# Top-k attention with a gated feed-forward: four units transposed by TensorE instead of by DMA

## The chip, the cores and the metric

One Trainium2 chip, one core. The metric is device time in microseconds (us), the median of three runs. The profile is one further execution, taken by the hardware profiler; its times are counted from the start of its span.

## The reference, cut to what matters

```python
# q, k, v: (8, 8, 576, 64);  w_in: (512, 2048);  w_out: (2048, 512)
scores = scale * q @ k.T
kth = np.partition(scores, -32, axis=-1)[..., -32:-31]   # 32nd largest of 576
scores = np.where(scores >= kth, scores, -1e9)
attn = exp(scores - max) ; attn = attn / (attn.sum + 1e-9)
x = (attn @ v).transpose(0, 2, 1, 3).reshape(4608, 512)
h = x @ w_in
out = (h * cos(h)) @ w_out
```

The two weight matrices arrive as 64-bit floats. The kernel reads them as pairs of 32-bit integers and decodes them itself.

## The kernel before, in words

**Units and slots.** The 4608 tokens are cut into 36 blocks of 128. For each block there are four *units*, one per pair of heads (NP is 4): 144 units. The main loop runs one *slot* per unit. In slot `i` three units are at work: `u` (unit i) is searched for its top 32 values, `w` (unit i-1) is masked and exponentiated, and `x` (unit i-2) is transposed. Every second slot, two older units `z` are multiplied with V.

**What each engine does in a slot.** VectorE folds the 576 scores to two halves (`fold_high`, L260) and runs eight rounds of MAX8 and MATCH_REPLACE8 (L352, L357); this is its main work. GpSimd makes the other half of the fold (L276, L285). For unit numbers in `BUSY` it does not: there VectorE makes it with one more instruction (`fold_now`, L268). Late in the slot VectorE takes the sum (L397) and the reciprocal (L402) of unit w's exponentials, which ScalarE made (mask L381, exponentials L389). ScalarE also copies the next unit's scores from PSUM (L248, and L252 for the last 128 columns, which lie in a tile called `rim`).

**Transposing a unit.** P@V needs the probabilities with the keys on the partitions. `send` does that by way of DRAM: `split` lets GpSimd rewrite the unit as 16-bit halves (L412) together with the reciprocals spread over 128 columns (L414), `write_halves` writes 640 KB to DRAM on SyncE's queue (L422), and `transposes` reads it back with a DMA transpose (L428) into `pT`. There is one `halves` buffer. `values` then makes P@V on TensorE (L447) into columns 256 to 383 of `rim`, and `take_values` multiplies it by the transposed reciprocals on VectorE (L455) into `xT`.

**Feed-forward.** When the four units of a block have their `xT`, the block's feed-forward may start: 8 pieces of the first product (`ff1`, L504) and 8 of the second (`ff2`, L579), 576 pieces in all. Between them stand two ScalarE reads of each bank (L518, L520), a range reduction on GpSimd (L540, L549), a sine on ScalarE (L559) and a gate on GpSimd (L566). `feed` hands pieces to TensorE between the attention products, about four a slot, limited by a credit. After the last slot only feed-forward work of the last blocks is left.

**Weights.** The 32 weight chunks of 512 KB are loaded during the first slots into staging buffers (seven of tag `g`, shared with the feed-forward, and three of tag `x`). Each is decoded in three steps: two ScalarE instructions at the end of a slot (L133, L136), one on VectorE in the next slot (L144), one on GpSimd behind it (L154), which frees the staging buffer. A piece may be issued only if the chunks that it needs were decoded in an earlier slot.

**Order.** Nothing is rescheduled: each engine's instructions stand in the order in which the program issues them, and each engine and each DMA queue works through its own in order. Slot 0 starts with L260 at 7.40 us; the start of a slot below is always the start of its L260.

Of the kernel before, what the change touches and what calls it, by code (L numbers as in the profile page):

```python
# [10 lines left out]
F32 = mybir.dt.float32  # L11
# [6 lines left out]
P = 128  # L18
# [12 lines left out]
def kernel(  # L31
# [9 lines left out]
    nc = tc.nc  # L41
    ctx.enter_context(tc.manual_schedule())
    B, H, D, S = qT.shape
    DM, DF = moe_w_in.shape
    NT = S // P
    TAIL = S - NT * P
    MAIN = NT * P
    NP = H // 2
# [8 lines left out]
    work = ctx.enter_context(tc.tile_pool(name="work", bufs=2))  # L57
    small = ctx.enter_context(tc.tile_pool(name="small", bufs=4))
    ps = ctx.enter_context(tc.tile_pool(name="ps", bufs=2, space=bass.MemoryType.PSUM))
# [3 lines left out]
    ident = consts.tile([P, P], F32, tag="ident")  # L63
# [15 lines left out]
    NC = DM // P  # L79
# [12 lines left out]
        w_out.append(w)  # L92
        chunks.append((moe_w_out[f * P : (f + 1) * P, :], w))
    CHUNKS, XB = 7, 3
    BUSY = range(7, 12)
    ff = {"live": 0, "tick": 0, "now": 0, "credit": 0.0, "end": False, "kind": 0, "half": 0, "open": 0, "late": False}

    wq = {"next": 0, "loaded": deque(), "second": deque(), "third": deque(), "done": 0, "ready": 0}
# [1 line left out]
    def staged(spare=0):  # L100
        return sum(c[2] == spare for k in ("loaded", "second", "third") for c in wq[k])

    def load_weights(n, queue):
        for _ in range(n):
            i = wq["next"]
            if i >= len(chunks):
                return
            src, dst = chunks[i]
            if not DECODE:
                queue.dma_start(out=dst, in_=src)  # L110
                wq["next"] = wq["done"] = i + 1
                continue
            spare = i < 3 * XB and i % 2 == 1 and staged(1) < XB
            if spare:
                st = ffw.tile([P, CW, 2], I32, tag="x", name="st", bufs=XB)
            elif staged() + ff["live"] >= CHUNKS:
                return
            else:
                st = ffw.tile([P, CW, 2], I32, tag="g", name="st", bufs=CHUNKS)
            queue.dma_start(out=st.rearrange("p w i -> p (w i)"), in_=src)  # L120
            wq["loaded"].append((st, dst, int(spare)))
            wq["next"] = i + 1
# [38 lines left out]
    units = []  # L161
# [61 lines left out]
    rim = ps.tile([P, 2, 512], F32, tag="rim", name="rim", bufs=1)  # L223
    sc_ends = [rim[:, :, i * (S - SB) : (i + 1) * (S - SB)] for i in range(2)]
    room = [rim[:, j, 2 * (S - SB) :] for j in range(2)]
# [28 lines left out]
    def fold_high(u):  # L254

        s, sc = u["s"], u["sc"]
        if u["n"] not in BUSY:
            del u["sc"]
# [5 lines left out]
    def fold_now(u):  # L264

        s, sc = u["s"], u.pop("sc")
        u["low"] = work.tile([P, 2, HS], F32, tag="low", name="low", bufs=1)
        nc.vector.tensor_tensor(  # L268
            out=u["low"], in0=sc[:, :, 0:HS], in1=s[:, :, HS:S], op=ALU.min
        )  # L270

    def fold_sum(u):

        s = u["s"].bitcast(I32)
        u["low"] = work.tile([P, 2, HS], F32, tag="low", name="low", bufs=1)
        nc.gpsimd.tensor_tensor(  # L276
            out=u["low"].bitcast(I32), in0=s[:, :, 0:HS], in1=s[:, :, HS:S], op=ALU.add
        )

    def fold_low(u):  # L280

        if u["n"] in BUSY:
            return
        low = u["low"].bitcast(I32)
        nc.gpsimd.tensor_tensor(  # L285
            out=low, in0=low, in1=u["rest"][:, :, HS:S].bitcast(I32), op=ALU.subtract
        )
# [15 lines left out]
    def topk_first(u, w):  # L303

        u["top"] = tops[u["n"] % len(tops)]
        if w:
            merge_first(w)
        if u["n"] not in BUSY:
            fold_sum(u)
        fold_high(u)  # L310
        if w:
            merge_second(w)
        if u["n"] in BUSY:
            fold_now(u)
        topk_round(u, 0, [lambda: bounds(w), lambda: distances(w)] if w else ())
# [21 lines left out]
    def merge_first(u):  # L337
        n = TOPK // 2 + 1
        u["lesser"] = u["top"].rearrange("p j r i -> p j (r i)")[:, :, 2 * n : 3 * n]
        nc.vector.tensor_reduce(  # L340
            out=u["lesser"], in_=u["top"][:, :, 0:n], axis=mybir.AxisListType.X, op=ALU.min
        )

    def merge_second(u):
        nc.vector.tensor_reduce(
            out=u["top"][:, :, TOPK - 1, 1], in_=u.pop("lesser"), axis=mybir.AxisListType.X,
            op=ALU.max,
        )
# [58 lines left out]
    def split(u):  # L407


        s = u.pop("s").rearrange("p j k -> p (j k)").bitcast(U16)  # L410
        halves = work.tile([P, 2, 2 * S + P], U16, tag="halves", name="halves", bufs=1)
        nc.gpsimd.tensor_copy(out=halves[:, :, 0 : 2 * S], in_=s.rearrange("p (k h) -> p h k", h=2))  # L412
        rden = u.pop("rden").bitcast(U16).rearrange("p (j h) -> p h j", h=2)
        nc.gpsimd.tensor_copy(  # L414
            out=halves[:, :, 2 * S :].rearrange("p h (j d) -> p h j d", j=2),
            in_=rden.unsqueeze(3).to_broadcast([P, 2, 2, D]),
        )
        u["halves"] = halves

    def write_halves(u):  # L420
        rows = u["rows"] = dram.tile([P, 2, 2 * S + P], U16, tag="rows", name="rows")
        nc.sync.dma_start(out=rows, in_=u.pop("halves"))  # L422

    def transposes(u):
        rows = u.pop("rows").rearrange("q h k -> (q h) k")
        pT = u["pT"] = work.tile([P, 2 * NT + 2, P], F32, tag="pT", name="pT", bufs=3)
        words = pT.rearrange("p c q -> p (c q)").bitcast(U16)
        nc.sync.dma_start_transpose(  # L428
            out=words.rearrange("p (c q) -> p c q", c=2 * NT + 2), in_=rows
        )  # L430
# [95 lines left out]
    def take_banks():  # L526
        while full:
            take, *what = full.popleft()
            take(*what)
# [22 lines left out]
    def sines(least):  # L552

        n = sum(c[3] < ff["now"] for c in waiting)
        if n == 0 or (n < least and waiting[0][3] + 2 > ff["now"]):
            return
        for _ in range(n):
            blk, g, x, _ = waiting.popleft()
            nc.scalar.activation(out=x, in_=x, func=AF.Sin, bias=halfpi, scale=TWO_PI_BELOW)  # L559
            sined.append((blk, g, x))  # L560
# [88 lines left out]
    at_slot, at_once = {}, {}  # L649
# [7 lines left out]
    for n in range(NP, len(order)):  # L657
        i = last[order[n - 6]] if n >= 6 else 0
        load_at(max(i, 2 * NP + 2), load_qk, *order[n])
        i = last_values[order[n - 6]] if n >= 6 else 0  # L660
        load_at(max(i + 4 - i % 2, 2 * NP + 2), load_v, *order[n])

    for hp in range(NP):
        at_once[hp] = [(load_v, 0, hp)]
    for hp in range(2, NP):
        at_once[hp - 2].append((load_qk, 0, hp))


    for i, u in enumerate(units):
# [2 lines left out]
    def send(x):  # L672

        split(x)
        write_halves(x)
        transposes(x)

    def slot(i, u, w, x, z):
        n = (3, 4, 3, 2)[i] if i < NP else 2 if i < 2 * NP else 3
        if i < NP:  # L680
            for load, b, hp in at_once[i]:
                load(b, hp)
        load_weights(n, nc.sync if i < 2 else nc.scalar)
        if x:
            send(x)
        decoding = i < 3 * NP
        ff["late"] = False
        topk_first(u, w)
        fold_low(u)
        topk_round(u, 1)  # L690
        topk_round(u, 2)
        if decoding:
            sines(1)
            gate(1)
        decode_second(NP)
        decode_third()
        reduce_first()
        reduce_second()
        made = scored.get(i, [])
        if z:  # L700
            take_banks()
        feed(1)

        for m in made:
            scores(m)
        if z:
            values(z)


        late = len(made) > 0  # L710

        if i % 2 and not decoding:
            sines(1)
        if w:
            mask(w)
        take_banks()
        if w and late:
            exponentials(w)
        if i + 1 < NU:
            take_scores(units[i + 1])  # L720
        if w and not late:
            exponentials(w)
        topk_round(u, 3, both(w), z)
        ff["late"] = not decoding
        if i in at_slot:
            load, b, hp = at_slot[i]
            load(b, hp)
        gate(1)
        feed(1 if len(made) == 2 else 2)
        take_banks()  # L730
        decode_first(NP)
        reduce_first()
        reduce_second()
        feed(1 if len(made) == 2 else 3)
# [31 lines left out]
    tt = ps.tile([P, 512], F32, tag="mm", name="warm", bufs=2)  # L766
# [8 lines left out]
    for i in range(NU):  # L775
        ff["credit"] = min(ff["credit"] + 5.0 - 0.9 * len(scored.get(i, [])), 5.3)
        ff["now"] += 1
        wq["ready"] = wq["done"]
        u, w, x = (units[i - n] if n <= i else None for n in range(3))
        z = units[i - 4 : i - 2] if i % 2 == 0 and i >= 4 else None  # L780
        slot(i, u, w, x, z)
    ff["end"], ff["late"] = True, False
    drain(units[NU - 1], units[NU - 2], units[NU - 4 : NU - 2])
# [42 lines left out]
```

## Time and profile before

| | |
|---|---|
| median of 3 runs | 1442.53 us (1441.97 to 1443.62) |
| the profiled execution's own time | 1443.18 us |
| its span, first to last instruction | 1441.4 us |
| mean granted TensorE clock | 0.993 |
| TensorE busy | 1371.2 us (95%) |
| VectorE busy | 1359.3 us (94%) |
| GpSimd busy | 1166.3 us (81%) |
| ScalarE busy | 1089.5 us (76%) |

Busy shares of the whole span mix three stages: a start of some 170 us in which weights are loaded and decoded and little feed-forward work is there, a long even stretch, and a last stretch of some 60 us with feed-forward work alone. Each has to be read by itself. The starts of the first slots in this execution, read from VectorE's timeline:

| slot | 0 | 1 | 2 | 3 | 4 | 5 | 6 | 7 |
|---|---|---|---|---|---|---|---|---|
| start, us | 7.40 | 17.22 | 27.21 | 37.66 | 48.34 | 63.01 | 72.67 | 82.73 |

| slot | 8 | 9 | 10 | 11 | 12 | 13 | 14 | 15 |
|---|---|---|---|---|---|---|---|---|
| start, us | 93.03 | 105.14 | 115.77 | 128.69 | 139.32 | 149.18 | 159.96 | 169.35 |

### The profile page before, as it was taken

The numbers are of one execution on the slowest core, as the hardware profiler recorded it, in microseconds if no ns is written. First come the engines' busy times: TensorE is split into PE (matmuls) and PEld (weight loads), VectorE is DVE, ScalarE is ACT, GpSimd is POOL, SyncE is SP. The second block draws the span as 40 slices with busy tenths as digits, with TensorE's granted clock in tenths as the row PEclk, the third lists the DMA queues.
The fourth block names the chain that finished last, engine by engine and source line by source line (L and its number), as shares of the span: only waits on it lengthen the run. The fifth ranks groups of instructions, "written<-read, shape, count | busy, mean of one in ns | idle before, by whom it ended". The sixth has DMA issues, their size and how long they took to land.

```text
span 1441.4 us, 30146 instructions
## 1 busy us (share of the span) xinstructions
PE 1371.2 (95%) x10252; PEld 978.4 (68%) x10252; DVE 1359.3 (94%) x5237; ACT 1089.5 (76%) x1910; POOL 1166.3 (81%) x816
## 2 busy tenths in 40 slices
PE   4387899999999999999999999999999999999998
PEld 3164677777777777777777777777777777777765
DVE  7899999999999999999999999999999999999931
ACT  7577787777777788777877777777877778777742
POOL 6876888888888888888888888888888888888820
PEclk9989999999999999999999999999999999999999
DMA  8877676666666566657665566756665656655530
GB/s 288 254 216 208 184 199 175 156 167 184 187 154 151 152 191 187 163 143 189 185 168 153 148 187 177 179 154 161 196 186 152 140 169 170 167 143 151 154 99 15
DMA packets 438379, 245.25 MB, mean 170 GB/s; under 512 B 386384, under 2 KB 403024, under 8 KB 438224
## 3 DMA queue, kind: packets, MB, share of 16 engines
q1 hardware_dynamic: 429648, 222.13, 57.6%
q10 hardware_dynamic: 8576, 21.19, 4.2%
q8 instruction: 81, 1.33, 0.4%
q14 instruction: 74, 0.61, 0.1%
HBM read 45.09 MB, written 103.81 MB: 103 GB/s over the span
## 4 chain that ended last, share of the span: by engine, by line
PE 88%; DVE 7%; ACT 3%; DMA 1%; SPq 0%; POOL 0%; issue 0%; ACTq 0%; POOLq 0%
PE mm L504 34%; PE o L579 33%; PE rim L447 11%; PE sc L238 8%; DVE top L352 3%; PE rim L238 2%; DVE rest L357 2%; DMA rows<-halves 1%; DVE rest L260 1%; ACT s L381 0%; DVE low L357 0%; ACT s L389 0%; SPq L428 0%; DVE w_out L144 0%; DMA pT<-rows 0%
## 5 line engine op out<-in xcount | busy, mean ns | idle before, releaser
L504 PEld LDWEIGHTS mm<-xT,w_in 128*128 128x128 f32 x4608 | 536.9, 192 | 76.4 <-issue 64.7
L504 PE MATMUL mm<-xT,w_in 128*128 128x128 f32 x4608 | 539.2, 275 | 8.0 <-ACT x L520 4.8
L579 PE MATMUL o<-w_out,g 128*128 128x512 f32 x1152 | 537.4, 600 | 9.4 <-POOL w_out L154 5.3
L352 DVE MAX8 top<-rest 128x8 f32<-128x288 f32 x1152 | 478.9, 451 | 0.0
L412 POOL COPY halves<-s 128x2304 uint16<-128x2304 uint16 x144 | 303.1, 2105 | 159.2 <-ACT s L389 153.4
L357 DVE MATCH_REPLACE8 rest<-top,rest 128x288 f32<-128x288 f32 x864 | 376.6, 443 | 0.0
L579 PEld LDWEIGHTS o<-w_out,g 128*128 128x128 f32 x1152 | 202.7, 190 | 197.3 <-issue 186.5
L352 DVE MAX8 top<-low 128x8 f32<-128x288 f32 x576 | 243.9, 449 | 2.7 <-POOL low L285 2.6
L389 ACT ACTIVATE s<-s,nd 128x576 f32<-128x576 f32 x288 | 220.2, 767 | 0.8
L285 POOL TENSOR_TENSOR low<-low,rest 128x576 int32<-128x576 int32 x139 | 197.2, 1418 | 10.9
L381 ACT ACTIVATE s<-s,top 128x576 f32<-128x576 f32 x288 | 206.0, 765 | 0.0
L276 POOL TENSOR_TENSOR low<-s 128x576 int32<-128x576 int32 x139 | 196.6, 1414 | 5.0 <-ACT s L252 5.0
L238 PE MATMUL sc<-k,q 64*128 64x448 f32 (+1 forms) x640 | 150.1, 588 | 35.4 <-DVE rest L260 16.3
L518 ACT ACTIVATE g<-mm 128x512 f32<-128x512 f32 x144 | 85.9, 596 | 118.0 <-PE mm L504 115.8
L549 POOL TENSOR_TENSOR x<-g,x 128x1024 f32<-128x1024 f32 x68 | 160.9, 2365 | 5.7
L566 POOL TENSOR_TENSOR g<-g,x 128x1024 f32<-128x1024 f32 x68 | 161.0, 2368 | 0.0
L447 PE MATMUL rim<-pT,v 128*64 128x128 f32 (+1 forms) x2560 | 148.6, 270 | 0.0
L447 PEld LDWEIGHTS rim<-pT,v 128*64 128x64 f32 x2560 | 130.8, 140 | 12.5 <-issue 11.3
L248 ACT COPY s<-sc 128x896 f32<-128x896 f32 x144 | 129.2, 898 | 3.6 <-PE sc L238 3.2
L252 ACT COPY s<-rim 128x256 f32<-128x256 f32 (+1 forms) x160 | 60.8, 380 | 90.2 <-PE rim L447 90.0
L357 DVE MATCH_REPLACE8 low<-top,low 128x288 f32<-128x288 f32 x288 | 125.5, 444 | 0.0
L260 DVE TENSOR_TENSOR rest<-sc,s 128x576 f32<-128x576 f32 x144 | 107.7, 748 | 6.3 <-ACT s L252 6.3
(47 smaller groups left out, 1196.9 us busy)
## 6 DMA issues: line engine op xcount, KB each, us to landing
rows<-halves SPq DMA_DIRECT2D x144, 640.0 KB, 3.0
out_dram<-ob ACTq DMA_DIRECT2D x36, 256.0 KB, 2.2
q<-in_q_dram SPq DMA_DIRECT2D x31, 288.0 KB, 3.4
v<-in_v_dram SPq DMA_DIRECT2D x32, 256.0 KB, 3.3
st<-in_moe_w_out_dram ACTq DMA_DIRECT2D x16, 512.0 KB, 4.6
st<-in_moe_w_in_dram SPq DMA_DIRECT2D x10, 512.0 KB, 5.4
k<-in_k_dram SPq DMA_DIRECT2D x31, 144.0 KB, 3.3
k<-in_k_dram SPq DMA_DIRECT2D x32, 128.0 KB, 3.4
```

The costliest lines, as they stand in the source:

```text
L238: nc.tensor.matmul(to[r0 : r0 + rows, rim_bank(r0, j) if k0 else place(u["hp"], j), 0 : k1 - k0], st["q"][d, q0 : q0 + rows], st["k"][d, k ...
L276: nc.gpsimd.tensor_tensor(out=u["low"].bitcast(I32), in0=s[:, :, 0:HS], in1=s[:, :, HS:S], op=ALU.add)
L285: nc.gpsimd.tensor_tensor(out=low, in0=low, in1=u["rest"][:, :, HS:S].bitcast(I32), op=ALU.subtract)
L352: nc.vector.max(to[:, j], src[:, j])
L357: nc.vector.match_replace(rest[:, j], to[:, j], src[:, j], NEG)
L381: nc.scalar.activation(out=s[:, j], in_=s[:, j], func=AF.Prelu, bias=less[:, j, 1:2], scale=1.0, alpha=FAR)
L389: nc.scalar.activation(out=s[:, j], in_=s[:, j], func=AF.Exp, bias=nd[:, j : j + 1], scale=SCALE, accum_out=den[:, j, 0:1],)
L412: nc.gpsimd.tensor_copy(out=halves[:, :, 0 : 2 * S], in_=s.rearrange("p (k h) -> p h k", h=2))
L447: nc.tensor.matmul(room[i][d, r], lhsT, rhs, start=c == NT, stop=c == NT - 1)
L504: nc.tensor.matmul(mm[:, at : at + w], w_in[f // FC][:, c, (f % FC) * P : (f % FC + 1) * P], blk["xT"][:, c], start=c == 0, stop=c == NC - 1,)
L566: eng.tensor_tensor(out=g, in0=g, in1=x, op=ALU.mult)
L579: nc.tensor.matmul(o, g[:, at : at + P], w_out[f], start=f == 0, stop=f == NF - 1)
```

## The change

Units 0 to 3 are no longer sent through DRAM. A new function `turn` lets TensorE transpose them into PSUM (nine 128x128 transposes) and makes the spread, transposed reciprocals as two products with the identity; ScalarE copies the results to `pT` in three instructions. `turn` runs in slots 2 to 5, in `send`'s place; `send` starts with unit 4 in slot 6. P@V of units 2 and 3 is made in slot 5 instead of slot 6. The weights go on SyncE's queue up to slot 5 (before: slot 1), and the numbers of chunks a slot are raised: with three ahead of the loop, the chunks whose VectorE step falls in slots 0 to 12 are 3, 3, 4, 3, 2, 2, 2, 2, 2, 3, 2, 3, 1 before and 3, 3, 4, 4, 3, 4, 3, 2, 2, 2, 2, 0, 0 after. The loads of V for the first four head pairs move from slots 0 to 3 to slots 2 and 3. Unit 11 leaves `BUSY`.

```diff
-    BUSY = range(7, 12)
+    BUSY = range(7, 11)
...
-            spare = i < 3 * XB and i % 2 == 1 and staged(1) < XB
+            spare = i < 2 * NC + 10 and i % 2 == 1 and staged(1) < XB
...
+    def turn(u):
+
+        s = u.pop("s").rearrange("p j k -> p (j k)")
+        pT = u["pT"] = work.tile([P, 2 * NT + 2, P], F32, tag="pT", name="pT", bufs=3)
+        for half in range(2):
+            tt = ps.tile([P, 512], F32, tag="mm", name="tt", bufs=2)
+            for c in range(NT):
+                at = (half * NT + c) * P
+                nc.tensor.transpose(tt[:, c * P : (c + 1) * P], s[:, at : at + P], ident)
+            nc.scalar.copy(out=pT[:, half * NT : (half + 1) * NT], in_=tt.rearrange("p (c q) -> p c q", c=NT))
+        at = 2 * NT * P
+        nc.tensor.transpose(room[0][:, P : 2 * P], s[:, at : at + P], ident)
+        rden = u.pop("rden")
+        for j in range(2):
+            lhsT = rden[:, j : j + 1].to_broadcast([P, D])
+            nc.tensor.matmul(room[1][j * D : (j + 1) * D, P : 2 * P], lhsT, ident, start=True, stop=True)
+        nc.scalar.copy(out=pT[:, 2 * NT :], in_=rim[:, :, 3 * P :])
...
-        at_once[hp] = [(load_v, 0, hp)]
+        at_once.setdefault(hp // 2 + 2, []).append((load_v, 0, hp))
     for hp in range(2, NP):
-        at_once[hp - 2].append((load_qk, 0, hp))
+        at_once[hp - 2] = [(load_qk, 0, hp)]
...
-        n = (3, 4, 3, 2)[i] if i < NP else 2 if i < 2 * NP else 3
+        n = (3, 4, 4, 3, 4, 3)[i] if i < NP + 2 else 2
...
-        load_weights(n, nc.sync if i < 2 else nc.scalar)
+        load_weights(n, nc.sync if i < NP + 2 else nc.scalar)
         if x:
-            send(x)
+            (turn if i < NP + 2 else send)(x)
...
         z = units[i - 4 : i - 2] if i % 2 == 0 and i >= 4 else None
+        if NP < i < NP + 3:
+            z = units[2:4] if i == NP + 1 else None
```

## The prediction

> **What bounds the kernel now.** I read the page's busy shares, then the chain that ended last, then a table by stretches cut at slot starts, then VectorE's waits and each engine's timeline in the first 170 us.
>
> ```profile
> PE 88%; DVE 7%; ACT 3%; DMA 1%; SPq 0%; POOL 0%; issue 0%; ACTq 0%; POOLq 0%
> ...
> 48.30:63.00 14.70, 7.21 (x48) 5.07 (x48) 10.48 (x40) 5.69 (x12) 11.23 (x9) 1.00 0.86 233
> 63.00:72.70 9.70, 1.82 (x8) 0.84 (x8) 9.70 (x39) 7.11 (x15) 6.29 (x6) 0.61 1.00 336
> 169.30:1370.00 1200.70, 1199.94 (x9163) 858.83 (x9163) 1187.62 (x4626) 945.43 (x1652) 1035.09 (x709) 1.00 0.62 168
> ```
>
> The columns of the last three are stretch, length, then busy time of TensorE, its weight loads, VectorE, ScalarE, GpSimd, then clock, DMA share and GB/s. From 169.3 to 1370 us TensorE is busy 1199.94 of 1200.70 us: it is the bound, and VectorE has 13 us to spare. Before 169 us TensorE has long gaps, and VectorE runs through: slot 5 is 9.70 of 9.70. Only slot 4 breaks that, 10.48 of 14.70. So two rules: a saving on TensorE before slot 14 is worth nothing by itself, and a VectorE stall there moves the moment from which TensorE never rests again. Comparing the two programs' orders on TensorE, 25 feed-forward pieces stand ahead of slot 14's P@V in both, and the order is the same from there to the end. The last stretch therefore holds the same work; what the change gives is how much earlier slot 14 starts (159.96 us now).
>
> The stalls on VectorE from slot 0 to 13:
>
> ```profile
> 43.40 2.27 POOL L285 TENSOR_TENSOR low<-low,rest 128x576 int32<-128x576 int32 x1
> ...
> 52.02 2.10 POOL L412 COPY halves<-s 128x2304 uint16<-128x2304 uint16 x1 [2.63 <-DMA rows<-halves]
> ...
> 57.69 0.82 DVE L352 MAX8 top<-low 128x8 f32<-128x288 f32 x2 [2.03 <-POOL low L285]
> ...
> 61.56 0.49 DVE L455 TENSOR_TENSOR xT<-rim,pT 128x128 f32<-128x128 f32 x2 [2.19 <-ACT s L252]
> ...
> 61.15 0.37 ACT L252 COPY s<-rim 128x256 f32<-128x256 f32 x1 [7.22 <-PE rim L447]
> ...
> 56.80 0.69 PE L447 MATMUL rim<-pT,v_tail 64*64 64x128 f32 x4 [4.75 <-DMA pT<-rows]
> 57.42 3.68 PE L447 MATMUL rim<-pT,v 128*64 128x128 f32 x32
> ...
> 89.01 0.75 DVE L144 TENSOR_SCALAR w_out<-w_out 128x512 int32<-128x512 int32 x2
> ...
> 122.04 2.99 DVE L144 TENSOR_SCALAR w_out<-w_out 128x512 int32<-128x512 int32 x2
> ...
> 122.22 2.53 POOL L566 TENSOR_TENSOR g<-g,x 128x1024 f32<-128x1024 f32 x1
> ```
>
> Slot 4 is the DRAM trip: the write of `halves` was late behind loads, so GpSimd waited 2.63 for the one buffer, its fold was late, and VectorE waited 2.03; then the DMA transpose held TensorE 4.75, P@V was late, L252 stands behind it, and VectorE waited 2.19. The last three lines are a hidden stall: two L144 take 0.75, but 2.99 while GpSimd's gate runs. Adding up: slot 3 0.57 (L285), slot 4 4.22, slot 8 1.33 (1.17 hidden in L144), slot 10 2.24, slot 12 0.13, slot 13 1.52 (L397 behind ScalarE): 10.0 us.
>
> **The change part by part.**
>
> *VectorE's own work.* The same 32 chunks and ten `xT` products up to slot 13; unit 11 leaves `BUSY`, one L268 less, 0.66 by the step between its neighbours. So gain = 0.66 + 10.0 - S, with S the stalls of the new order. Bare slots: 9.0 (slot 14: 9.39 with 0.40 for `xT`), plus 0.33 a chunk, 0.40 with `xT`, 0.66 in `BUSY`.
>
> *Removed.* Four L412/L414 pairs on GpSimd (2.5 us each), four 640 KB writes and transposes, so SyncE no longer stands 7 us on a write in slots 2 and 3. The stalls of slots 3 and 4 lose their causes.
>
> *Added: turn.* Neither the transposes of `s` nor the products with the identity are in the trace. Nearest rows: the 12 warm-up transposes, 2.82 us, 0.235 each; P@V cold, 3.68/32, two records a product, 0.23; ScalarE's L518 (512 columns from PSUM, 0.48 step) and L252 (256 columns, 0.27). Nine and two make 2.6 us on TensorE, three copies 1.25 on ScalarE. Lower bound: nothing exposed (a gain is excluded, it is extra work); upper: all 3.9 in each of four slots, 15 us. I step it. The products wait for L402, the end of the slot before; the last copy is then done some 1.2 us into the slot, and the mask behind it waits for VectorE's L372, 1.7 us into it. ScalarE's slot is 4.0 (mask 1.43, exponentials 1.53, copies 1.06) plus 1.12 a chunk plus 1.25: 9.7 with four chunks, under VectorE's 10.3. Cover: VectorE; without it, 1.25 a slot.
>
> *A rule against it.* The trace has P@V at 1.97 us when TensorE had been busy and 3.68 when not, though the granted clock is printed as 1.00 in both. The Trainium skill, "TensorE: Matmul & The Clock Gate", Part 4: PE-mode transpose, says that transposes do not count as busy for the clock gate. By that rule P@V behind `turn` stays cold, 4.3 with its tails; if transposes warmed the array, 2.3. The sums differ by S in slot 5: 0.7 against none. No row here decides; I take cold.
>
> *Loads.* Up to slot 5 some 16 MB on SyncE's queue. The kernel moves 321 to 357 GB/s in slots 0 and 1. The V loads stand behind weights and Q/K and land by 40 us, wanted at 52. Chunk 17 waits for a staging buffer freed by L154 of slot 3 (about 48.7); four chunks at 260 GB/s land by about 58, and ScalarE wants them from 57.5 to 61. Cost nothing, cover 2 to 3 us. Later chunks on ScalarE's queue wait for buffers freed earlier.
>
> *Stepped by hand from slot 4.* Start 48.1 = 7.40 + 9.82 + 9.99 + 10.45 + 10.11 + 0.33. Slot 5 at 58.5 (three chunks, `xT`).
> Slot 4: TensorE cold: products 0.5, scores 5.0, P@V 4.3 from 48.0, say 57.5 to 57.8; L252, four chunks (4.5), copies: 63.5. Slot 5: P@V until 67.8 (VectorE wants it at 68.1), L252 and exponentials 69.6, L397 wants them at 68.9: 0.7. Slot 6 at 69.9.
> Slot 6: GpSimd makes four L154 until 70.5, L412/L414 until 73.0, folds until 75.9; L144 comes at 75.5 and waits 0.4. Two bank reads stand ahead of the exponentials, so L252 ends at 80.6: 0.4 more. Slot 7 at 80.7.
> Slot 7: three L154 until 80.8, L540 and L549 until 84.2, L412/L414 until 86.6, the first gate until 89.0. L144 comes at 87.0: 2.0. Slot 8 at 93.0.
> Slot 8: the second product waits for that gate; five pieces of 1.8 (the chain has 32 records of L504, two pieces, in 3.57) from 89.0 to 98.0 (99.5 if cold), scores and P@V to 102.9 or 104.4, wanted at 102.3: 0.6 to 2.1, I take 1.3.
> Slot 9: gate about 108.4 to 110.8, L144 at 111: 0.3. Slots 10 to 13: no gate beside L144, the sine of slot 13 not late: none.
> S = 0.7 + 0.8 + 2.0 + 1.3 + 0.3 = 5.1. Gain 5.6; slot 14 at 154.4.
>
> *The second rule.* L144 at 2.99 beside L566, and L285 stretched from 1.41 to 2.27 beside L144. The skill's "SBUF — State Buffer", SBUF: two separate sides, says that GpSimd and a two-port VectorE instruction hold a port pair exclusively for a whole instruction, whoever starts first. By the rule each L144 that starts inside any GpSimd instruction waits for its end: 0.4 + 2.0 + 0.3. Were only the gate's collisions real, 2.3. The rows bear the rule out; since arrivals are known to about 1 us, slots 6 to 9 together could be 0 to 6.
>
> *The sum.* 1443.18 - 5.6 = 1437.6 for the profiled execution, whose median lies 0.65 lower: 1437.0.
>
> **The rivals.**
> *Collisions and waits eat the gain.* The first gate comes a slot earlier, and chunks are packed three and four a slot, so GpSimd is behind in slots 6 and 7 (12.5 us of work in slot 6). If slots 6 to 10 meet a GpSimd instruction at full length and slot 13 keeps its 1.5, S is 8 to 13 and the time 1440 to 1445. For it: two of five L144 groups beside feed-forward work were hit before. Against: that takes nearly every one.
> *Cleaner than stepped.* L144 falls between GpSimd's instructions and the array is warm: S about 2, 1433.8. Against: the gate follows `split` directly, 4.9 us of GpSimd without a hole.
> *Slower: weights late in front of turn.* In slots 4 and 5 ScalarE's order is chunks, copies, mask, L252 behind P@V, exponentials, and VectorE's L397 waits for the last. Every us that chunk 20 lands after 61 is a us of stall. It is slower by 0.2% (2.9 us) only from S above 10.7 + 2.9, some 13.5, 8.4 more than stepped: chunk 20 would have to land after about 69.5, 2.1 MB in 21 us or 100 GB/s. For it: all loads in one queue, each waiting for a staging buffer. Against: 336 GB/s in slot 5 before.
> *The change doesn't do what it says:* the orders show that it does.
>
> **How the numbers follow.** As stepped, S 3 to 7.8: 0.66. Cleaner, S below 3: 0.14. Eaten, S 7.8 to 13.5: 0.13. Slower: 0.07. About 2.9 us (0.2%) is what a measurement of this kernel can tell from no change. The likeliest time is 1437.0. The range, 1433.5 to 1441.0, is S from 1.6 to 9.1. Faster 0.80, same 0.13, slower 0.07.
>
> **What would show it.** Right: slot 5 starts near 58.5 and slot 14 near 154.4; no wait for L285 in slots 3 and 4; L144 long in slot 7. Wrong: L397 or `xT` waiting several us in slots 5 to 8; ScalarE waiting for staging loads after 50 us; TensorE idle after slot 15, which would show that the shift is not kept to the end.

## The result and the profile after

| | before | after |
|---|---|---|
| median of 7 runs each, same chip | 1442.83 us (1441.97 to 1449.78) | 1438.23 us (1436.85 to 1439.10) |
| ratio, after to before | | 0.9960, 95% interval 0.9943 to 0.9976 |
| profiled execution, its own time | 1443.18 us | 1438.41 us |
| its span | 1441.4 us | 1436.6 us |
| start of slot 5 | 63.01 us | 58.41 us |
| start of slot 14 | 159.96 us | 154.32 us |

The change makes the kernel faster by 0.3 to 0.4%: the quotient of the two medians is 0.9968, and the ratio in the table, 0.9960, is that of the means, into which one run of 1449.78 us before enters. In the experiments, too, the ratio can differ from the quotient of the medians, by up to 0.0005. The forecast, 1437.0 within 1433.5 to 1441.0 and faster with 0.80, holds.

The new kernel is 18 lines longer behind `turn`: P@V is now L465 (before: L447), `xT` L473 (L455), the first product L522 (L504), the gate L584 (L566), the second product L597 (L579), the write to DRAM L440 and the DMA transpose L446.

The same views as before. The chain that ended last, in shares by engine:

```profile
PE 87%; DVE 10%; ACT 1%; POOL 1%; DMA 1%; issue 0%; POOLq 0%
```

The table by stretches; its columns are stretch, length, busy time of TensorE, its weight loads, VectorE, ScalarE and GpSimd, clock, DMA share and GB/s.

```profile
48.02:58.41 10.39, 7.78 (x71) 5.22 (x71) 10.39 (x41) 8.57 (x18) 8.20 (x7) 0.83 0.82 317
58.41:69.13 10.72, 6.82 (x54) 5.60 (x55) 10.72 (x42) 8.37 (x18) 6.56 (x6) 0.66 0.29 88
...
163.70:1364.40 1200.70, 1199.00 (x9154) 857.92 (x9153) 1186.37 (x4621) 944.50 (x1651) 1032.80 (x707) 1.00 0.63 168
```

Slot 4 (the first row) was 14.70 us long with VectorE busy for 10.48; now it is 10.39 and VectorE is busy for all of it. The chain runs over VectorE for longer at the start (10% where it was 7%) and less over ScalarE (1% where it was 3%). The last row has the same length as the long stretch shown before: TensorE is again busy without a hole, but for 1.7 us where it was 0.8.

What is left of VectorE's stalls, in its timeline, with the instruction behind each. The columns are start, duration, engine, line, operation, tiles and, in brackets, the idle time before it and what ended it:

```profile
74.50 1.40 POOL L285 TENSOR_TENSOR low<-low,rest 128x576 int32<-128x576 int32 x1
74.78 2.08 DVE L144 TENSOR_SCALAR w_out<-w_out 128x512 int32<-128x512 int32 x3
...
80.47 0.76 DVE L260 TENSOR_TENSOR rest<-sc,s 128x576 f32<-128x576 f32 x1 [0.27 <-ACT s L252]
...
86.61 2.35 POOL L584 TENSOR_TENSOR g<-g,x 128x1024 f32<-128x1024 f32 x1
86.76 2.83 DVE L144 TENSOR_SCALAR w_out<-w_out 128x512 int32<-128x512 int32 x2
...
104.02 0.37 ACT L252 COPY s<-rim 128x256 f32<-128x256 f32 x1 [2.57 <-PE rim L465]
104.42 0.49 DVE L473 TENSOR_TENSOR xT<-rim,pT 128x128 f32<-128x128 f32 x2 [2.25 <-ACT s L252]
```

Three L144 take 1.08 us elsewhere and 2.08 here; two take 0.75 elsewhere and 2.83 beside the gate. With the one wait in slot 8, the measured S is 0 in slot 5, 1.3 in slot 6, 2.1 in slot 7, 2.25 in slot 8 and 0 from slot 9 on: 5.6 us, where 5.1 was stepped.

Of the 5.64 us by which slot 14 starts earlier, the span shows 4.8. The rest went in slot 18:

```profile
189.39 3.04 SPq L446 DMA_TRANSPOSE pT<-rows  x1
...
197.74 0.43 PE L465 MATMUL rim<-pT,v_tail 64*64 64x128 f32 x4 [0.95 <-DMA pT<-rows]
```

This DMA transpose landed 8.3 us after its issue, against a median of 5.0, and TensorE waited 0.95 us for it.

### The profile page after: what moved, and what is told of

It reads as the page before. It is cut to its first block, busy times and chain, and to the rows that moved or that the text cites. A ratio compares the mean times of both kernels' runs of the same rounds, so it can differ in the third digit from the quotient of the medians.

```text
span 1436.6 us, 30243 instructions
## 1 busy us (share of the span) xinstructions
PE 1379.4 (96%) x10304; PEld 984.4 (69%) x10304; DVE 1357.6 (95%) x5236; ACT 1093.7 (76%) x1922; POOL 1158.1 (81%) x810
## 4 chain that ended last, share of the span: by engine, by line
PE 87%; DVE 10%; ACT 1%; POOL 1%; DMA 1%; issue 0%; POOLq 0%
PE o L597 34%; PE mm L522 33%; PE rim L465 11%; PE sc L238 8%; DVE top L352 4%; DVE rest L357 3%; PE rim L238 2%; DVE rest L260 1%; DVE low L357 1%; DMA pT<-rows 1%; DVE w_in L144 0%; DVE w_out L144 0%; POOL w_out L154 0%; DVE top L340 0%; DVE xT L473 0%
## 5 line engine op out<-in xcount | busy, mean ns | idle before, releaser
L522 PEld LDWEIGHTS mm<-xT,w_in 128*128 128x128 f32 x4608 | 538.2, 192 | 74.3 <-issue 64.3
L597 PE MATMUL o<-w_out,g 128*128 128x512 f32 x1152 | 541.2, 604 | 17.0 <-POOL g L584 16.2
L522 PE MATMUL mm<-xT,w_in 128*128 128x128 f32 x4608 | 540.5, 276 | 6.9 <-DVE xT L473 5.2
L412 POOL COPY halves<-s 128x2304 uint16<-128x2304 uint16 x140 | 294.5, 2104 | 161.9 <-ACT s L389 156.5
L597 PEld LDWEIGHTS o<-w_out,g 128*128 128x128 f32 x1152 | 204.7, 192 | 208.4 <-issue 190.9
L285 POOL TENSOR_TENSOR low<-low,rest 128x576 int32<-128x576 int32 x140 | 197.6, 1412 | 11.0
L584 POOL TENSOR_TENSOR g<-g,x 128x1024 f32<-128x1024 f32 x68 | 160.8, 2365 | 0.8 <-ACT x L577 0.8
L465 PE MATMUL rim<-pT,v 128*64 128x128 f32 (+1 forms) x2560 | 146.1, 267 | 0.0
L465 PEld LDWEIGHTS rim<-pT,v 128*64 128x64 f32 x2560 | 128.3, 138 | 12.2 <-issue 11.1
L252 ACT COPY s<-rim 128x256 f32<-128x256 f32 (+1 forms) x160 | 60.8, 380 | 89.0 <-PE rim L465 88.8
```

The source lines that it names most:

```text
L285: nc.gpsimd.tensor_tensor(out=low, in0=low, in1=u["rest"][:, :, HS:S].bitcast(I32), op=ALU.subtract)
L465: nc.tensor.matmul(room[i][d, r], lhsT, rhs, start=c == NT, stop=c == NT - 1)
L522: nc.tensor.matmul(mm[:, at : at + w], w_in[f // FC][:, c, (f % FC) * P : (f % FC + 1) * P], blk["xT"][:, c], start=c == 0, stop=c == NC - 1,)
L597: nc.tensor.matmul(o, g[:, at : at + P], w_out[f], start=f == 0, stop=f == NF - 1)
```

## The experiments

In all of them one quantity is read from VectorE's timeline, the time from the start of slot 0 to the start of slot 14. It is 152.56 us before and 146.77 after. From there to the end of the span there are 1280.9 to 1282.3 us in every kernel here, though slot 14 starts anywhere from 151.1 to 167.4. So what a version is worth is settled before slot 14, as the prediction had it. But one profile is one execution: the whole change, profiled twice, has 146.77 and 148.29 us, and its version with P@V in slot 6 has 148.27 and 145.41. Below, differences are therefore read slot by slot as well.

**The turn alone, P@V of units 2 and 3 in slot 5.** Weights, V loads and `BUSY` as before:

```diff
 # the kernel before, with turn added
-            send(x)
+            (turn if i < NP + 2 else send)(x)
...
+        if NP < i < NP + 3:
+            z = units[2:4] if i == NP + 1 else None
```

> Only the TensorE transposes and P@V of units 2 and 3 in slot 5; weights, V loads, staging and BUSY as before. Theory: the gain is the end of the DRAM trip's stalls (4.8 us in slots 3 and 4); chunks only move VectorE work between slots. Then slot 14 starts at 154.5 to 156.5 (159.96 before, 154.32 with the whole change) and the time is 1438 to 1440. Rival, the faster weights are what lets the feed-forward start early: the transposes alone give under 1.5 us, slot 14 after 158.5, 1441.5 or more.

Measured: 1441.51 us median against 1442.63, ratio 0.9996 (0.9987 to 1.0006): no difference. Slot 14 starts at 160.39 us, 153.62 us after slot 0. The DRAM trip's stalls are gone, so that slots 3 and 4 are together 5.3 us shorter than before, but more came back. In slot 2 the sum of the exponentials waits:

```profile
31.54 0.67 ACT L133 ACTIVATE w_in<-st 128x512 f32<-128x512 f32 x1 [2.40 <-DMA st<-in_moe_w_in_dram]
...
39.95 0.16 DVE L397 TENSOR_REDUCE den<-dens 128x2 f32<-128x4 f32 x1 [1.88 <-ACT s L389]
...
81.09 0.16 DVE L397 TENSOR_REDUCE den<-dens 128x2 f32<-128x4 f32 x1 [0.88 <-ACT s L389]
...
100.42 2.17 DVE L144 TENSOR_SCALAR w_out<-w_out 128x512 int32<-128x512 int32 x2
```

ScalarE waited 2.40 us for a late weight chunk; turn's copies, the mask and the exponentials stand behind it on ScalarE. With late chunks in slots 0 and 1 too, slots 0 to 2 are 4.0 us longer than before. Further stalls came in slots 6, 7 and 8, some 5.6 us together, where feed-forward work now meets weight chunks; the stall of slot 10 is gone, and slots 5 to 10 are together 2.4 us longer than before. My theory, that the removed trip is the gain, fell, and the numbers that the rival named came true. How much of it is due to P@V in slot 5, the next run tells.

**The same with P@V of units 2 and 3 left in slot 6.** The lines with `z` above are left out; all else is as in the last kernel.

> The kernel before with the turn of units 0 to 3 and nothing else: weights, V loads, BUSY as before, and P@V of units 2 and 3 left in slot 6. It stands beside the first experiment, which had them in slot 5. My theory (the first experiment lost its gain because the feed-forward began a slot early, while weights were still being decoded): the stalls of slots 6 to 8 (5.6 us there) go, those of slots 8, 10 and 13 of the kernel before (5.1 us) come back, slot 2's stall stays; slot 14 between 157.5 and 159, time 1440.0 to 1441.0. Rival (the slow weights and slot 2's stall cost it wherever P@V stands): as the first experiment, 1441 to 1442. Second rival (slot 2's stall was bad luck of the loads): 1438 to 1439.5.

Measured: 1438.68 us against 1442.16, ratio 0.9980 (0.9971 to 0.9989); slot 14 at 157.41, 150.01 us after slot 0. Slot 2's stall is there again:

```profile
39.43 0.16 DVE L397 TENSOR_REDUCE den<-dens 128x2 f32<-128x4 f32 x1 [1.82 <-ACT s L389]
...
96.84 1.93 DVE L144 TENSOR_SCALAR w_out<-w_out 128x512 int32<-128x512 int32 x2
...
119.50 3.00 DVE L144 TENSOR_SCALAR w_out<-w_out 128x512 int32<-128x512 int32 x2
...
156.71 0.16 DVE L397 TENSOR_REDUCE den<-dens 128x2 f32<-128x4 f32 x1 [1.51 <-ACT s L389]
```

Slots 6 and 7 are without a stall, and in slots 8, 10 and 13 stand exactly the stalls of the kernel before. Slots 5 to 10 are together as long as before. So P@V in slot 5 cost the first experiment 2.4 us there. The rest of what it lost, 4.0 us in slots 0 to 2, is no matter of P@V: here too these slots are 2.8 us longer than before. Slot 14 came out 0.1 us ahead of the span of my theory; the median is 1.3 us below that span, in the span of the second rival. But the profiled execution (1441.16) was among the slowest of eleven, and slot 2's stall had returned in it. How often it comes in the timed runs isn't known.

**The weights alone.** Everything but `turn`: all units through DRAM, P@V of units 2 and 3 in slot 6, with the new weight plan, V loads and `BUSY`.

```diff
 # the whole change
-            (turn if i < NP + 2 else send)(x)
+            send(x)
...
-        if NP < i < NP + 3:
-            z = units[2:4] if i == NP + 1 else None
```

> Only the weights, the V loads, the staging and BUSY as changed; all units through DRAM, P@V of units 2 and 3 in slot 6. Theory: the stalls of slots 3 and 4 stay, and the loads in front of the writes on SyncE's queue make them longer; slot 14 at 160 to 166, time 1443 to 1449. Rival, weights: slot 14 at 156 or earlier, 1439.

Measured: 1449.25 us, ratio 1.0043 (1.0028 to 1.0058), slot 14 at 167.42, 160.66 us after slot 0: my theory in kind, but slot 14 is 1.4 us later than its span. Where it goes, in slots 4 to 6:

```profile
55.96 2.57 POOL L412 COPY halves<-s 128x2304 uint16<-128x2304 uint16 x1 [4.25 <-DMA rows<-halves]
...
61.74 0.82 DVE L352 MAX8 top<-low 128x8 f32<-128x288 f32 x2 [4.43 <-POOL low L285]
...
72.62 3.83 DVE L144 TENSOR_SCALAR w_out<-w_out 128x512 int32<-128x512 int32 x4
...
89.44 0.69 PE L465 MATMUL rim<-pT,v_tail 64*64 64x128 f32 x4 [5.92 <-DMA pT<-rows]
...
94.01 0.49 DVE L473 TENSOR_TENSOR xT<-rim,pT 128x128 f32<-128x128 f32 x2 [3.54 <-ACT s L252]
```

The first two lines are slot 4's stall of the kernel before (2.63 and 2.03 us there), now longer: the write of `halves`, issued on SyncE's queue at 48.15 behind the loads, had landed only at 55.9, against a median of 3.0 us from issue to landing. The third is slot 5, where four L144 that take 1.42 elsewhere take 3.83 beside GpSimd's late work. The last two are slot 6, where P@V waits for the DMA transpose as it did in slot 4. Slots 3 to 6 are together 13.0 us longer than before, of which 1.7 are chunks moved there; slots 7 to 13 are 5.3 shorter. The early weights pay only because `turn` takes the trip through DRAM out of their way.

**The whole change with P@V of units 2 and 3 in slot 6**, run twice, the second time beside the whole change itself:

```diff
 # the whole change
-        if NP < i < NP + 3:
-            z = units[2:4] if i == NP + 1 else None
```

> The whole change, but P@V of units 2 and 3 back in slot 6. Theory: what counts is only when slot 14 starts, with 25 feed-forward pieces ahead of it in either order; the first gate moves to slot 8, where only two chunks wait on VectorE, so the collision of slot 7 (2.1 us hidden in L144) and the wait of slot 8 (2.25) are changed for some 1.2 each in slots 8 and 10 and up to 1.5 in slot 13: slot 14 at 153 to 155, the time within 1.5 us of the whole change. Rival, the earlier feed-forward is worth its slot: 3 us or more slower than the whole change.

> The third experiment's kernel once more, beside the whole change in one call, because its four timed runs spread by 5.5 us. Theory (P@V in slot 5 or 6 makes no difference of its own: the same sum of stalls, moved): within 1 us of the whole change, 1437 to 1439. Rival (P@V in slot 6 is better because the first gate meets fewer weight chunks): 1435 to 1436.5, 2 us under the whole change.

> The whole change once more on the chip of the three others, as their measure. Both theories: 1437.5 to 1439; slot 14 at 154.0 to 155.0, and a tail from there of 1281 rather than 1282.3, if the late DMA transpose of slot 18 was an accident of the first profile.

Measured: 1435.59 us (four runs, 1434.22 to 1439.73), ratio 0.9952 (0.9936 to 0.9969), and again 1435.12 (five runs, 1433.84 to 1436.92), ratio 0.9956 (0.9944 to 0.9969). The whole change beside it: 1438.57 (1437.05 to 1440.33), ratio 0.9977 (0.9968 to 0.9986). In this second comparison P@V in slot 6 is 3.45 us better, and no run of the one overlaps those of the other. My theories, that it would make no difference beyond 1.5 or 1 us, were wrong. The timelines say why. With P@V in slot 6, the engines in slot 8:

```profile
95.82 1.97 PE L465 MATMUL rim<-pT,v 128*64 128x128 f32 x32
...
96.01 2.37 POOL L584 TENSOR_TENSOR g<-g,x 128x1024 f32<-128x1024 f32 x1
...
97.05 1.95 DVE L144 TENSOR_SCALAR w_out<-w_out 128x512 int32<-128x512 int32 x2
...
98.43 3.70 PE L597 MATMUL o<-w_out,g 128*128 128x512 f32 x8 [0.65 <-POOL g L584]
```

and in the whole change, run again:

```profile
86.22 3.00 DVE L144 TENSOR_SCALAR w_out<-w_out 128x512 int32<-128x512 int32 x2
...
88.99 6.68 PE L597 MATMUL o<-w_out,g 128*128 128x512 f32 x8 [6.43 <-POOL g L584]
...
103.35 1.97 PE L465 MATMUL rim<-pT,v 128*64 128x128 f32 x32
...
105.77 0.49 DVE L473 TENSOR_TENSOR xT<-rim,pT 128x128 f32<-128x128 f32 x2 [3.96 <-ACT s L252]
```

With P@V one slot later, the gate of block 0 ends after slot 8's P@V has begun. TensorE runs the first product without a gap up to the scores, P@V follows at once, and the second product comes after it. In the whole change the second product stands ahead of P@V, begins on an array that has rested 6.43 us, and takes 6.68 us for eight records (granted clock 0.55) where the other order takes 3.70 (clock 1.00). The stalls add up to 3.0 us (0.57 in slot 6, 1.2 in each of slots 8 and 10) against 7.2 (1.0 in slot 6, 2.25 in slot 7, 3.96 in slot 8). Of these 4.2 us the two profiles show 2.9 at slot 14, since slot 0 happened to be 1.2 us longer in the profile with P@V in slot 6. The rival had the size; its reason, fewer weight chunks at the first gate, is the smaller part: what is hidden in L144 falls only from 3.25 to 2.4 us, and the wait for `xT`, 3.96, goes altogether. In the first profiled execution of this version, the slowest of its four, the stall in slot 8 was 3.30: a DMA transpose issued at 86.64 landed 13 us later, and TensorE waited 5.56 for it. The second profiled execution doesn't have it.

In the whole change run again, 1280.9 us lie between slot 14 and the end: the 0.8 us of slot 18 did not return. Slot 8's stall was 3.96 instead of 2.25, so that the span is 1436.6 once more.

**Unit 4 transposed by TensorE too**, with P@V of units 2 and 3 in slot 6:

```diff
-            (turn if i < NP + 2 else send)(x)
+            (turn if i < NP + 3 else send)(x)
```

> The version with P@V of units 2 and 3 in slot 6, and unit 4 also transposed by TensorE in slot 6, so that the DRAM trip begins with unit 5. In that version GpSimd's two rewrites of unit 4 (2.5 us) stood ahead of the fold for which VectorE waited 0.57 us in slot 6. My theory (GpSimd's queue in slot 6 is what that wait is for): the wait is gone, the rest is unchanged, 0.6 us earlier at slot 14, 1434.5 to 1435.5. Rival (ScalarE, which gets 1.25 us of copies behind two bank reads in slot 6, is the tighter engine there): the exponentials of slot 6 come late, VectorE's L397 or L252 waits 0.5 to 1.5 us, and the time is 1435.6 to 1437.

Measured: 1434.75 us (1434.50 to 1435.08), ratio 0.9954 (0.9942 to 0.9967). The wait for L285 in slot 6 is gone, and slot 6 is 10.38 us long instead of 11.06; slot 14 starts 143.72 us after slot 0, the least of all and 1.7 less than in the version with four units; 1.0 of that is a shorter slot 0. It is the best version that was run, 3.8 us under the whole change. Against the version with four units, 0.37 us lie within the spread of that one's runs, so that step shows in the trace and not surely in the time.

**Unit 11 back in `BUSY`.**

```diff
-    BUSY = range(7, 11)
+    BUSY = range(7, 12)
```

> The whole change, but unit 11 in BUSY again, so that VectorE makes its fold. Theory: slot 11 longer by 0.66 us, slot 14 at 155.0, and nothing else changed up to there; the time 0.7 us longer, too little for the timing to show. Rival: GpSimd, with two instructions less, frees something and the time falls.

Measured: slot 11 is 9.63 us long instead of 8.99, so 0.64 for the one L268, as stepped (0.66). Slot 14 starts at 155.73 instead of the 155.0 expected, with 3.25 us of wait for `xT` in slot 8. The median, 1438.62 us with ratio 0.9971 (0.9962 to 0.9980), can't show so little.

**Does a transpose warm the array?** Forty more transposes, or 24 products of the same operands, behind `turn` in slot 5:

```diff
                 nc.tensor.transpose(tt[:, c * P : (c + 1) * P], s[:, at : at + P], ident)
+            for _ in range(40 if u["n"] == 3 and half == 1 else 0):
+                nc.tensor.transpose(tt[:, 0:P], s[:, 0:P], ident)
 # in the other kernel:
+            for _ in range(24 if u["n"] == 3 and half == 1 else 0):
+                nc.tensor.matmul(tt[:, 0:P], s[:, 0:P], ident, start=True, stop=True)
```

> The whole change, and in slot 5, behind the P@V of slot 4, TensorE makes 40 more transposes of unit 3 (their results are written over by the real ones), some 5.5 us of them, so that it is not idle ahead of the P@V of slot 5. By the skill's rule that transposes don't keep the clock gate open, that P@V's 32 records still take 3.7 us and the later transposes fall to the slow step of 0.23 us; if they count as any matmul, 2.0 us and 0.13 us throughout. Slot 14 within 1 us of the whole change either way.

> The same with 24 plain products with the identity in the place of the 40 transposes, some 5.4 us. Both views expect the array kept warm: the 32 records of slot 5's P@V take 2.0 us. If they take 3.7 here too, the gap of under 1 us between the products and P@V is what cools it, and the pair decides nothing.

TensorE's timeline in slot 5 and the table by stretches there, first of the whole change, then of the kernel with the transposes:

```profile
61.39 3.68 PE L465 MATMUL rim<-pT,v 128*64 128x128 f32 x32
```

```profile
60.60:65.10 4.50, 4.45 (x41) 3.83 (x41) 4.50 (x17) 2.17 (x4) 0.93 (x1) 0.51 0.00 0
```

```profile
54.96 4.53 PE L427 MATMUL tt<-ident,s 128*128 128x128 f32 x40
...
61.41 1.97 PE L467 MATMUL rim<-pT,v 128*64 128x128 f32 x32
```

```profile
55.00:59.50 4.50, 4.50 (x44) 4.50 (x42) 4.50 (x20) 4.50 (x8) 4.50 (x4) 1.00 0.37 117
61.41:63.38 1.97, 1.97 (x35) 1.80 (x33) 1.97 (x9) 1.64 (x3) 0.00 (x0) 1.00 0.04 8
```

Forty transposes take 4.53 us, 0.113 each, at a granted clock of 1.00, and P@V behind them takes 1.97 us instead of 3.68, just as behind the 24 products (5.52 us, then 1.97). So transposes do keep a warm array warm here. The printed clock alone would not settle it, since in the kernel before it stood at 1.00 while P@V took 3.68; the durations do. Whether transposes alone would warm a cold array was not tried. That was not what decided slot 5: VectorE had no stall there in either. The times, one run each, are 1436.54 and 1437.55 us; they are too few to tell them from the whole change.

**The gate of slots 7 and 9 on VectorE**, which takes GpSimd's gate from beside L144:

```diff
-            eng = nc.vector if ff["end"] else nc.gpsimd
+            eng = nc.vector if ff["end"] or ff["now"] in (8, 10) else nc.gpsimd
```

> The whole change, with the gate of slots 7 and 9 on VectorE (1.23 us at the kernel's end) instead of GpSimd. Theory: L144 of slot 7 then finds GpSimd idle: 2.1 us hidden in it go, 1.23 us of gate come, and the gate is done about 1 us earlier, so that P@V of slot 8 waits 1 us less; slot 9 pays 1.23 for nothing. Slot 14 at 153.5 to 154.5, the time within 1 us of the whole change. Rival, L144's 2.83 us is no collision but its own cost in that place: it stays long, and slot 14 comes at 156.5 or later.

```profile
87.40 1.32 DVE L584 TENSOR_TENSOR g<-g,x 128x1024 f32<-128x1024 f32 x1
88.65 0.75 DVE L144 TENSOR_SCALAR w_out<-w_out 128x512 int32<-128x512 int32 x2
```

L144 is back at 0.75, so the long L144 is the gate's doing. But VectorE pays 1.32 for the gate itself, L397 then waits 0.90, `xT` in slot 8 still waits 2.63, and slot 9 is 1.1 us longer for its gate. Slot 14 came at 156.67, not at 153.5 to 154.5; 1.1 us of that were lost in slot 0 already. That is where the rival put it, but not for its reason. 1438.02 us, ratio 0.9967 (0.9954 to 0.9979): no gain over the whole change that shows.

**V loads as before**, in slots 0 to 3, in the whole change:

```diff
-        at_once.setdefault(hp // 2 + 2, []).append((load_v, 0, hp))
+        at_once[hp] = [(load_v, 0, hp)]
...
-        at_once[hp - 2] = [(load_qk, 0, hp)]
+        at_once[hp - 2].append((load_qk, 0, hp))
```

> The whole change, but the V loads of the first four head pairs back in slots 0 to 3, ahead of the weights and Q/K there. Theory, from the run with the transposes alone: these 1.2 MB and 12 descriptors ahead in the queue make the chunks of slot 1 late; ScalarE's L133 waits 2 us for them, turn's copies, mask and exponentials stand behind, and L397 of slot 2 waits 1.5 to 2.5 us: slot 14 at 156 to 157.5, the time 1439.5 to 1441. Rival, the V loads don't matter: slot 2 runs 10.3 us and slot 14 comes within 0.7 us of 154.3.

Measured: 1439.21 us, ratio 0.9976 (0.9966 to 0.9987). ScalarE waits up to 3.01 us for a chunk in slots 0 and 1, and slot 2 still has no stall (10.33 us), against my theory. Slot 14 starts at 155.58; the 1.26 us by which slot 14 is later than in the first profile of the whole change come from slot 8 (`xT` 3.83), which by itself goes from 2.25 to 3.96. So the V loads alone do not make slot 2's stall of the two turn-only kernels. Two more things differ there, the chunks on ScalarE's own queue from slot 2 and the rule for the staging buffers, and the traces clear both: the late chunk is the eighth, which gets the same buffer by either rule, and ScalarE's queue issued its first chunk only at 34.29 and 33.76 us, after the waits. SyncE's queue issued the chunks of slot 1 at 22.76 and 22.59 us in those two runs, and at 20.00 in the kernel before and 20.84 here, with the same loads ahead of them. What delays them stays open.

## Why the prediction was right

*The frame* held: what is saved before slot 14 counts only as VectorE's start of slot 14. The signs named for a right forecast came: slot 5 at 58.41, no wait for L285 in slots 3 and 4, L144 long in slot 7. One of those for a wrong one came in part, the 2.25 us for `xT` in slot 8.

*The sum.* Stepped gain 5.6 us, slot 14 at 154.4; measured 5.64 and 154.32. That it came so close is luck, for the terms agree less well than the sum:

| | stepped | measured |
|---|---|---|
| slot 5, L397 behind a cold P@V | 0.7 | 0 |
| slot 6, L144 beside L285, then L252 | 0.8 | 1.3 |
| slot 7, L144 beside the gate | 2.0 | 2.1 |
| slot 8, `xT` | 1.3 | 2.25 |
| slot 9, L144 beside the gate | 0.3 | 0 |
| S | 5.1 | 5.6 |

With S at 5.6 the prediction's formula gives a gain of 0.66 + 10.0 - 5.6 = 5.1 us, and 5.64 were measured. So the old stalls were undercounted too. The lengths of the slots against their bare lengths give some 10.9 us for them instead of 10.0 (4.6 in slot 4 instead of 4.2, 1.7 in slot 13 instead of 1.5, and 0.1 more in each of slots 2, 3 and 8), and 5.8 for S. The two misses, 0.9 and 0.7 us, all but cancel.

*Slot 5.* P@V was cold, 3.68 us, as chosen, but it cost nothing. The step that failed lies in slot 4: it had P@V there cold and done by 57.5. It ran warm, right behind the scores, and was done by 54.4:

```profile
52.45 1.97 PE L465 MATMUL rim<-pT,v 128*64 128x128 f32 x32
```

So ScalarE got to its copies and masks 3 us sooner, slot 5's exponentials were done at 67.0, and L397 wanted them at 68.45.

*The rule on transposes.* The prediction took from the Trainium skill, "TensorE: Matmul & The Clock Gate", Part 4, that transposes don't count as busy, and so 0.7 us in slot 5. The result, cold, was what the rule gives, but for another reason. In slot 5 TensorE rested 2.15, 0.46 and 1.60 us between the few transposes and P@V; with forty more in that place P@V was warm. So it was the rest and not their kind, and the page's statement does not hold for these transposes. Whether they run in the transpose mode that the page means, the trace doesn't say: it lists them as MATMUL. Had the array been warm, the sum would have stood 0.7 lower, in the range either way.

*The rule on the shared port.* What the Trainium skill says in "SBUF — State Buffer", SBUF: two separate sides, was borne out where it counts: 2.83 beside the gate, 0.75 once the gate was on VectorE. In slot 6 the fold ended at 75.9 as stepped, but L144 came 0.7 us earlier, so it waited 1.0 instead of 0.4. The version with P@V in slot 6 shows the other order: L144 started first, at 75.06, and L285, which takes 1.40 alone, took 2.26:

```profile
75.16 2.26 POOL L285 TENSOR_TENSOR low<-low,rest 128x576 int32<-128x576 int32 x1
```

In slot 9 the gate had ended at 111.55, ahead of L144 at 112.15, and the 0.3 us did not come.

*Slot 8.* Stepped 0.6 to 2.1, with the upper end for a cold array. It was cold in part, hence 2.25:

```profile
89.02 5.30 PE L597 MATMUL o<-w_out,g 128*128 128x512 f32 x8 [4.66 <-POOL g L584]
```

Eight records take 3.70 us warm. In the second profile the array was cold nearly throughout (6.68), hence 3.96. The term, 1.3, was undersized by one to three us.

*The rivals.* "Collisions eat the gain" did not come true as a whole (of its 12.5 us of work for GpSimd in slot 6, 10.2 were there), but its mechanism, the first gate a slot earlier, is the largest loss in the change: P@V in slot 6 is 3.45 us faster. "Cleaner than stepped" is what that version shows, with S at 3.0. "Slower: weights late in front of turn" did not happen: in slots 4 to 6 ScalarE waited for no staging load. What the loads can do was seen where the copies of `turn` stood behind a late chunk (slot 2, 1.88 us) and, without `turn`, in the weights alone (6.6 us slower). The prediction took the parts of the change as terms of one sum. They are not: turn with P@V in slot 6 gives 3.5 us, the weights by themselves cost 6.6, both together give 7.0, and P@V in slot 5 takes 3.45 of that back.

## What to carry to other kernels

Removing a trip through DRAM is worth at most what its stall cost, and beyond that what else may then use the queue: here the second was as large as the first, and worth less than nothing without it. An early start of a chain is no gain by itself; look where its first consumer will land, on a shared port and in front of what somebody waits for. Where the start of one slot sets the end, step the engines slot by slot to that point and read the versions by the length of each slot: that told 0.6 us apart where the runs' spread is 3. The total up to that point is a coarser measure, for it moved by 1.5 and 2.9 us between two executions of one kernel.

## What the runs showed of the hardware

Transposes of 128x128 in float32 ran at 0.113 us each back to back on a warm array, and kept it warm for 4.5 us; 0.235, the figure of the warm-up row, was a cold one. A DMA transpose with a median of 5.0 us from issue to landing took 8.3 and 13 us at single places of two executions, and each time TensorE waited for it. Slot 1 started at 16.8 to 18.4 us in kernels that issue the same work up to slot 4, as the first chunks landed sooner or later; what makes them land so is open.
